# Other spare matmuls and another place for one group of products at the head of a fused mLSTM and two-layer MoE kernel

## The chip, the cores and the metric

The kernel runs on one core of a Trainium2 chip. The metric is the device time of one execution in microseconds. A run of the kernel before gives one time; the three that are known are 431.34, 433.4 and 435.36 us, the median is 433.4. One further execution was taken by the profiler; its span, from the first to the last instruction, is 429.5 us.

## The reference

An mLSTM runs over 768 steps for 2 batches of 8 heads with head size 40; its output, as 1536 tokens of 320 features, goes through two pairs of dense layers, 320 by 2048 and 2048 by 320, the first with a squared hinge, the second with a softplus.

```python
m_new = np.maximum(f_gate[:, :, t] + m, i_gate[:, :, t])
f_stab = np.exp(f_gate[:, :, t] + m - m_new)
i_stab = np.exp(i_gate[:, :, t] - m_new)
C = f_stab * C + i_stab * np.einsum('bhd,bhe->bhde', vt, kt)
n = f_stab * n + i_stab * kt
y[:, :, t] = sigmoid(o_gate) * einsum(C, qt) / maximum(abs(n . qt), 1)
...
g = np.where(h >= 1, h, np.where(h <= -1, 0.0, (h + 1) ** 2 / 4))     # h = x @ w_in
x = g @ w_out
...
g = np.maximum(h, 0.0) + np.log1p(np.exp(-np.abs(h)))                 # h = x @ w_in2
out = g @ w_out2
```

Inputs and outputs are float32. The weights arrive as 64-bit words and are turned into floats on the chip.

## The kernel before

The sequence is cut into 12 chunks of 64 steps; a chunk of both batches is 128 tokens. The maxima m come from two scans over the gates (L341): 256 steps (chunks 0 to 3, the early ones) and 512 steps (chunks 4 to 11, the late ones). For an early chunk the forget gates, a row for each head, are laid under a mask (`m`, L556), spread over 128 partitions by one product with `sel` (the spread, `bc`, L564) and turned into a triangular matrix of decays `f` by a scan on VectorE (L590). For a late chunk `f` comes by DMA from a scratch tensor (`scr_f`, L572) and is scanned at L598. `late` is the tile of the late chunks' gates; sixteen small products L422 (eight in the program, each in two passes), called the late maxima here, spread their maxima into bank D, three VectorE operations (L428) take them in, L432, L436 and L441 finish them, and two DMAs (L445) store them as `scr_d` and `scr_f`. The decay rows `dec` of the early chunks are stored from `gd` (L393) and read back on ScalarE's queue (L581).

A chunk's attention is, on TensorE, the scores (`qkp`, L518), the value product (`pv`, L505), the product with the state (`inner`, L511), the state's update (`stp`, L526) and three transposes of the result (L687); on VectorE the scores times the decays (L620), the query times the decay rows (L625), the denominator (L650, L653), the gated output (L657, L660), the state (L678) and the rest `xl` that the rounding to fp32r leaves (L698, L700); on GpSimd the scaled values `vi` and `ve` (L603, L613) and the state's decay (L669). `isp` (L399) are transposes that bring the input gates to the partitions.

The tokens form three blocks of 512 (chunks 0 to 3, 4 to 7, 8 to 11). A layer takes, for each of the 16 slices f of the hidden size, eight products up (L767), a few element operations, and eight products down (L836 to L842; in the second layer twelve, L897 to L899). Each weight slice comes as `raw` (L709), is turned into floats on ScalarE (L715, L719) and VectorE (L726) and split into two fp32r parts `w` (L738, L747); `raw` has two buffers, so a slice is fetched once VectorE is done with the one before the last. The first product needs chunks 0 to 3 and the first slice.

While TensorE has nothing to do in the head, it runs fills (L460): 128x512 bf16 products of a constant, whose result nobody reads.

The order on every engine is made by a planner, the class Plan, when the program is built: each piece of work is added with a cost, its reads and writes, a due time or a place `at`, and Plan.run goes through time by its own estimates and emits what is ready and most urgent. It keeps its own idea of TensorE's clock (fast or not, `self.fast`, with `self.edge` the next moment at which it may change). Fills are taken when no other TensorE work begins within 0.15 us by that clock; once the idea is fast, and fills and products of the last WINDOW sum to more than KEEP of it, a fill is left out and the engine left free for IDLE. After the first product no more are emitted. A task's `hold` is the planner's time before which it isn't chosen; on the chip nothing waits for it. What the chip does wait for are the data, and the order: each engine takes its instructions in the order in which they were emitted.

## Time and profile before

| | |
|---|---|
| median of three runs | 433.4 us (431.34 to 435.36) |
| span of the profiled execution | 429.5 us |
| TensorE (PE) busy | 409.7 us, 95% |
| VectorE (DVE) busy | 295.2 us, 69% |
| ScalarE (ACT) busy | 260.1 us, 61% |
| GpSimd (POOL) busy | 37.2 us, 9% |
| share of the chain that ended last | PE 77%, DMA 8%, DVE 6%, ACT 4% |

The time of the profiled execution itself, with what lies around its span, is not given; only the span is. PE is TensorE's products, PEld its weight loads, which overlap the products. Ends of products are modelled, so a row for several products is a little longer than the distance to the next one. "SPq" and "ACTq" are the queues of SyncE and ScalarE where DMAs are issued. A wait in brackets is the idle time of that engine in front of the row and what ended it.

### The profile page before, as it was taken

Reading aid. Unit: us, or ns where it says so; the run is one execution under the profiler, and the core shown is the slowest. Engines: PE = TensorE matmul, PEld = TensorE weight load, DVE = VectorE, ACT = ScalarE, POOL = GpSimd, SP = SyncE. Lnnn points to the kernel's source line nnn. Section 1 sums busy time; section 2 is a strip of 40 time slices with the busy share of each in tenths; the row PEclk is TensorE's granted clock in tenths of the full one; section 3 lists DMA queues with packets and bytes.
Section 4 is the critical chain, followed back from the end, with each engine's and each line's share of the span. In section 5 each row is a group of like instructions: output and inputs, shape, how many; then the busy total and the mean of one; then the engine's idle time right before and its main releaser. Section 6 shows DMA issues by size and latency. Waiting matters only on the chain.

```text
span 429.5 us, 8096 instructions
## 1 busy us (share of the span) xinstructions
PE 409.7 (95%) x3299; PEld 340.3 (79%) x3299; DVE 295.2 (69%) x479; ACT 260.1 (61%) x447; POOL 37.2 (9%) x46
## 2 busy tenths in 40 slices
PE   7988779999899999999999999999999999999994
PEld 5555558877788888887888888999989999899994
DVE  4687998999868556556878787655565555655552
ACT  3255867768666446889889755555555555555551
POOL 3333122213101000000000000000000000000001
PEclk9999969999999999999999999999999999999999
DMA  8979595797912001644344000000020000110002
GB/s 289 343 260 318 156 295 177 213 321 221 304 66 74 2 2 51 193 162 136 134 134 137 0 2 0 1 2 0 2 61 2 0 2 0 36 27 2 0 2 61
DMA packets 13685, 44.93 MB, mean 105 GB/s; under 512 B 2320, under 2 KB 3984, under 8 KB 13648
## 3 DMA queue, kind: packets, MB, share of 16 engines
q1 hardware_dynamic: 12832, 43.22, 31.2%
q10 hardware_dynamic: 752, 1.03, 0.9%
q8 instruction: 26, 0.43, 0.4%
q0 software_dynamic: 64, 0.16, 0.2%
q14 instruction: 11, 0.09, 0.1%
HBM read 42.36 MB, written 2.05 MB: 103 GB/s over the span
## 4 chain that ended last, share of the span: by engine, by line
PE 77%; DMA 8%; DVE 6%; ACT 4%; issue 1%; SPq 1%; POOL 0%; DVEq 0%; POOLq 0%
PE h L767 36%; DMA raw<-in_w_dram 5%; PE D L841 4%; PE D L840 4%; PE D L842 4%; PE D L897 3%; PE D L899 3%; PE D L898 3%; PE A L898 3%; PE A L899 3%; PE A L897 3%; PE D L836 2%; PE D L837 2%; DMA f<-scr_f 2%; ACT v L715 1%
## 5 line engine op out<-in xcount | busy, mean ns | idle before, releaser
L767 PE MATMUL h<-xh,w 128*128 128x512 f32 x576 | 182.6, 400 | 1.5 <-DVE w L747 1.1
L767 PEld LDWEIGHTS h<-xh,w 128*128 128x128 f32 x576 | 108.7, 189 | 26.8 <-DVE w L747 3.0
L820 DVE TENSOR_TENSOR gl<-u,gh 128x512 fp32r<-128x512 f32 x96 | 67.5, 704 | 39.6 <-ACT gh L816 38.4
L816 ACT CAST gh<-u 128x512 fp32r<-128x512 f32 x96 | 59.4, 619 | 46.7 <-DVE u L807 34.0
L767 PE MATMUL h<-xl,w 128*128 128x512 f32 x192 | 76.3, 397 | 1.4 <-DVE xl L698 1.4
L807 DVE TENSOR_TENSOR u<-u,e 128x512 f32<-128x512 f32 x48 | 33.3, 693 | 29.2 <-ACT e L803 29.2
L803 ACT ACTIVATE e<-e 128x512 f32<-128x512 f32 x48 | 30.3, 632 | 37.6 <-DVE e L798 37.6
L775 ACT ACTIVATE u<-h 128x512 f32<-128x512 f32 x48 | 28.5, 595 | 25.9 <-PE h L767 25.6
L767 PEld LDWEIGHTS h<-xl,w 128*128 128x128 f32 x192 | 36.4, 190 | 8.0 <-DVE xl L698 1.8
L784 DVE SCALAR_TENSOR_TENSOR u<-u,h 128x512 f32<-128x512 f32 x48 | 32.7, 682 | 13.9 <-ACT u L780 13.7
L841 PE MATMUL D<-gh,w 128*128 128x512 f32 x96 | 37.9, 395 | 0.0
L840 PE MATMUL D<-gh,w 128*128 128x512 f32 x96 | 37.8, 394 | 0.0
L842 PE MATMUL D<-gl,w 128*128 128x512 f32 x96 | 37.5, 391 | 0.0
L798 DVE SCALAR_TENSOR_TENSOR e<-u,h 128x512 f32<-128x512 f32 x48 | 33.0, 687 | 6.0 <-ACT u L794 1.0
L726 DVE SCALAR_TENSOR_TENSOR v<-raw,v 128x704 int32<-128x704 int32 x32 | 28.6, 895 | 9.8 <-ACT v L719 8.8
L794 ACT ACTIVATE u<-h 128x512 f32<-128x512 f32 x48 | 28.7, 598 | 10.6 <-PE h L767 10.3
L747 DVE TENSOR_TENSOR w<-v,w 128x64 fp32r<-128x64 f32 (+2 forms) x45 | 30.2, 701 | 2.4 <-ACT w L738 2.4
L715 ACT ACTIVATE v<-raw 128x704 f32<-128x704 int8 x32 | 27.1, 849 | 7.3 <-DMA raw<-in_w_dram 5.4
L780 ACT ACTIVATE u<-u 128x512 f32<-128x512 f32 x48 | 30.2, 630 | 0.4
L897 PE MATMUL D<-w,gh 128*128 128x320 f32 x96 | 29.6, 309 | 0.1
L899 PE MATMUL D<-w,gl 128*128 128x320 f32 x96 | 29.7, 309 | 0.0
L898 PE MATMUL A<-w,gh 128*128 128x320 f32 x96 | 29.7, 309 | 0.0
(120 smaller groups left out, 611.5 us busy)
## 6 DMA issues: line engine op xcount, KB each, us to landing
raw<-in_w_dram SPq DMA_DIRECT2D x32, 704.0 KB, 4.8
qx<-in_qk_dram SPq DMA_DIRECT2D x12, 640.0 KB, 7.2
tok<-in_tok_dram SPq DMA_DIRECT2D x12, 496.0 KB, 6.0
dec<-scr_d SPq DMA_DIRECT2D x16, 128.0 KB, 6.7
f<-scr_f SPq DMA_DIRECT2D x16, 128.0 KB, 6.7
out_dram<-o SPq DMA_DIRECT2D x20, 80.0 KB, 2.1
dec<-scr_d ACTq DMA_DIRECT2D x6, 128.0 KB, 7.0
consts<-in_ident_dram SPq DMA_DIRECT2D x1, 164.0 KB, 4.0
```

The costliest lines, as they stand in the source:

```text
L767: nc.tensor.matmul(hp, a, x, start=(i == 0), stop=(i == len(ops) - 1))
L784: nc.vector.scalar_tensor_tensor(out=tiles[U], in0=tiles[U], scalar=1.0, in1=tiles[HP], op0=ALU.min, op1=ALU.max)
L798: nc.vector.scalar_tensor_tensor(out=new("e", E, [128, n]), in0=tiles[M], scalar=-2.0, in1=tiles[HP], op0=ALU.mult, op1=ALU.add)
L807: nc.vector.tensor_tensor(out=tiles[M], in0=tiles[M], in1=tiles[E], op=ALU.add)
L816: nc.scalar.copy(new("gh", GH, [128, n], F32R), tiles[G])
L820: nc.vector.tensor_tensor(out=new("gl", GL, [128, n], F32R), in0=tiles[G], in1=tiles[GH].bitcast(F32), op=ALU.subtract)
L840: nc.tensor.matmul(d[i], hi[:, k], gh, start=s, stop=False)
L841: nc.tensor.matmul(d[i], lo[:, k], gh, start=False, stop=False)
L842: nc.tensor.matmul(d[i], hi[:, k], gl, start=False, stop=e)
L897: nc.tensor.matmul(d, gh[:, k], hi, start=s, stop=False)
L898: nc.tensor.matmul(d, gh[:, k], lo, start=False, stop=False)
L899: nc.tensor.matmul(d, gl[:, k], hi, start=False, stop=e)
```

## The change

Six lines of the planner's numbers and of two tasks' descriptions change; what is computed, and by which instructions, doesn't, but for the number of fills.

```diff
-    KEEP, IDLE = 0.8, 0.1
+    KEEP, IDLE = 1.1, 0.1
+    WARMUP = 6.9
...
-        self.fast, self.busy, self.edge = False, 0.0, self.WINDOW
+        self.fast, self.busy, self.edge = False, -1.0, self.WARMUP - self.WINDOW
...
-        ready = [t["hold"] for t in ts]
+        ready = [max(t["hold"], 0.0 if t["fill"] or t["eng"] != "pe" else self.WARMUP) for t in ts]
...
-    add("pe", 0.9, t, duty=0.75, reads=[(gm, 1), (gm, 0), (gi, 1), (("bc", 1),)], writes=[(("D",), "s")], at=-50.5)
+    add("pe", 1.75, t, duty=0.75, reads=[(gm, 1), (gm, 0), (gi, 1), (("bc", 1),)], writes=[(("D",), "s")], at=-50.5, hold=8.3)
...
-        add("pe", 0.25, t, fill=True, reads=[(("warm",),)], writes=[(("fill",),)], new=[("hb", ("fill",))] if i == 0 else [])
+        add("pe", 0.22, t, fill=True, reads=[(("warm",),)], writes=[(("fill",),)], new=[("hb", ("fill",))] if i == 0 else [])
```

By the planner's time no TensorE work but fills begins before 6.9; its idea of the clock may turn fast at 3.49 and then at 6.9; with KEEP at 1.1 no fill is ever left out; the late maxima cost it 1.75 in place of 0.9 and aren't chosen before 8.3. From these numbers the planner makes a new order on all engines. The number of fills goes from 40 to 54. From the third slice of block 1 on TensorE's order is what it was. The line added moves all later lines by one: L422 before is L423 after.

At the head of TensorE's order, behind five fills, there stood before (`qx_151` and `qx_157` are chunks 0 and 1, `bc_224` and `bc_256` their spreads):

```order
L518 MATMUL A<-qx_151 64x64 x16
L399 MATMUL isp_200<-consts,gi 128x16 x2
L422 MATMUL D<-gm,gi 128x65 x8
L460 LDWEIGHTS warm
L460 MATMUL fill<-warm 128x512
L564 MATMUL bc_224<-m_216,sel 128x512
```

and there stand now, behind nine fills and with three fills ahead of the first row (`bc_234` is the spread of chunk 0):

```order
L423 MATMUL D<-gm,gi 128x65 x8
L565 MATMUL bc_234<-m_216,sel 128x512
L519 MATMUL D<-qx_157 64x64 x16
L461 LDWEIGHTS warm
L461 MATMUL fill<-warm 128x512
```

The transposes `isp` and the scores of chunk 0 changed places ahead of those three fills. The late maxima stand directly ahead of the first spread, as before with a fill between. Four fills follow the last product shown, then the second spread.

On VectorE, from the third scan of a spread on, there stood before (`f_366` and `f_381` are chunks 2 and 3, `dec_120` and `dec_121` the decay rows of chunks 1 and 2):

```order
L590 SCALAR_TENSOR_TENSOR f_366<-bc_337,id_h 128x512
L657 SCALAR_TENSOR_TENSOR sig_339<-den_345,sig_339 128x320
L660 TENSOR_TENSOR y_372<-A,sig_339 128x320
L590 SCALAR_TENSOR_TENSOR f_381<-bc_374,id_h 128x512
L625 TENSOR_TENSOR qx_157<-qx_157,dec_120 128x512
L620 TENSOR_TENSOR f_366<-A,f_366 128x512
L625 TENSOR_TENSOR qx_220<-qx_220,dec_121 128x512
```

and there stand now (`f_310` and `f_362` are chunks 2 and 3):

```order
L591 SCALAR_TENSOR_TENSOR f_362<-bc_354,id_h 128x512
L658 SCALAR_TENSOR_TENSOR sig_351<-den_348,sig_351 128x320
L661 TENSOR_TENSOR y_384<-A,sig_351 128x320
L626 TENSOR_TENSOR qx_157<-qx_157,dec_120 128x512
L437 SCALAR_TENSOR_TENSOR late<-late 128x64
L442 MEMSET late 128x1
L621 TENSOR_TENSOR f_310<-A,f_310 128x512
L626 TENSOR_TENSOR qx_214<-qx_214,dec_121 128x512
```

The same operations stand ahead of the first L626, but for two masks (L557), which now stand earlier; the scan and the memset of the late rows moved from behind the second one to between the two. In the same order the 512-step scan of the maxima now stands ahead of the last two subtractions of the early gates, and the masks of chunks 1 and 2 ahead of the first scan of a spread (that of chunk 3 is on GpSimd).

On TensorE, behind the up products of slices 0, 1 and 2 of block 0, there stood before the down products of slice 0 and then chunk 4's attention; now there is this, and the down products of slice 1 follow (`f_548` is chunk 4, `w_0_578` slice 0):

```order
L506 MATMUL A<-vi_705,f_548 64x41 x16
L512 MATMUL A<-state,qx_439 64x41 x16
L519 MATMUL A<-qx_580 64x64 x16
L527 MATMUL A<-ve_725,tok_491 40x41 x16
L837 MATMUL D<-gh_0_0_738,w_0_578 128x512
L838 MATMUL D<-gl_0_0_758,w_0_578 128x512
```

Chunk 4's attention moved ahead of the first down products, and sixteen down products stand between it and its transposes, where none stood. On VectorE the scan of chunk 4 moved ahead of the first hinge.

## Rows read from the trace of the kernel before

**Rows 1.** Busy time by stretch (instructions in brackets), granted clock, DMA share
```profile
core 0: us, PE busy (x) PEld busy (x) DVE busy (x) ACT busy (x) POOL busy (x), PEclk, DMA share, GB/s
17.06:39.35 22.29, 18.74 (x458) 12.51 (x458) 20.89 (x44) 11.85 (x25) 9.19 (x11) 1.00 0.91 300
39.35:58.10 18.75, 13.49 (x171) 9.96 (x172) 15.46 (x27) 13.42 (x22) 3.27 (x3) 0.95 0.66 213
58.10:118.00 59.90, 57.75 (x712) 46.17 (x712) 54.28 (x95) 44.02 (x77) 12.78 (x14) 0.96 0.81 250
56.20:56.40 0.20, 0.00 (x0) 0.00 (x0) 0.17 (x2) 0.00 (x0) 0.00 (x0) 0.63 1.28 377
63.00:63.10 0.10, 0.10 (x2) 0.09 (x1) 0.10 (x1) 0.10 (x2) 0.00 (x0) 0.60 1.36 394
```

**Rows 2.** Chain of work that ended last, in time: start us, us, what
```profile
6.73 3.49 PE D L422 x16
...
11.19 1.31 PE fill L460 x3
...
16.48 0.75 PE fill L460 x3
...
22.46 0.67 PE A L518 x32
```

**Rows 3.** Timeline, TensorE: start us, us, line, operation, [idle before, what ended it]
```profile
1.92 2.32 PE L460 MATMUL fill<-warm 128*128 128x512 bf16 x5 [1.92 <-POOL warm L454]
...
39.35 0.50 PE L767 MATMUL h<-xl,w 128*128 128x512 f32 x1 [1.36 <-DVE xl L698]
...
50.01 0.68 PE L505 MATMUL A<-vi,f 64*64 64x41 f32 x32 [1.96 <-DVE f L620]
...
57.19 0.90 PE L687 MATMUL A<-consts,y 128*128 128x128 f32 x3 [2.85 <-DVE state L678]
```

**Rows 4.** Timeline, VectorE and, in the first row, ScalarE
```profile
4.99 0.41 ACT L369 ACTIVATE gi<-gi 16x256 f32<-16x256 f32 x1 [2.49 <-DVE gi L365]
5.22 1.27 DVE L341 TENSOR_TENSOR_SCAN gm<-gf,gm,gi 16x512 f32<-16x512 f32 x1
...
11.22 1.22 DVE L590 TENSOR_TENSOR_SCAN f<-bc,id_h 128x512 f32<-128x512 f32 x1 [2.67 <-PE bc L564]
...
14.56 1.22 DVE L590 TENSOR_TENSOR_SCAN f<-bc,id_h 128x512 f32<-128x512 f32 x1 [2.12 <-PE bc L564]
...
17.06 0.69 DVE L620 TENSOR_TENSOR f<-A,f 128x512 f32<-128x512 f32 x1 [0.74 <-ACT state L676]
17.67 1.28 DVE L556 TENSOR_TENSOR m<-gr,consts 128x512 fp32r<-128x512 f32 x2
...
22.90 0.67 DVE L625 TENSOR_TENSOR qx<-qx,dec 128x512 f32<-128x512 f32 x1
...
24.37 0.68 DVE L625 TENSOR_TENSOR qx<-qx,dec 128x512 f32<-128x512 f32 x1
...
27.55 0.28 DVE L436 TENSOR_TENSOR_SCAN late<-late 128x64 f32<-128x64 f32 x1
...
27.95 0.89 DVE L726 SCALAR_TENSOR_TENSOR v<-raw,v 128x704 int32<-128x704 int32 x1
...
29.90 0.42 DVE L698 TENSOR_TENSOR xl<-D,xh 128x256 fp32r<-128x256 f32 x1 [0.60 <-ACT xh L693]
...
42.58 0.69 DVE L784 SCALAR_TENSOR_TENSOR u<-u,h 128x512 f32<-128x512 f32 x1 [2.04 <-ACT u L780]
```

**Rows 5.** Decay rows' DMAs (L581): first two, then all four; issue and landing
```profile
L581 ACTq DMA_DIRECT2D dec<-scr_d x2: 520/561/602, 12.7 to 13.2; - x2
...
DMA to landing us min/median/max: 6.1/7.0/8.0
L581 ACTq DMA_DIRECT2D dec<-scr_d x4: 520/604/662, 12.7 to 14.6; - x4
...
DMA to landing us min/median/max: 6.1/8.6/9.3
```

## What I predict

> **What bounds the kernel now.** I read the page first: TensorE (PE) is busy 95% of a span of 429.5 us and three quarters of the chain that ended last are PE's. That is an average. From the third weight of block 1 on, some 126 us into the span, the change leaves the order of PE's work as it was, so it can act only before that. I therefore cut the time up to 118 us, behind which PE has work without a break, in three [rows 1]. From 17.06 to 39.35 VectorE (DVE) works 20.89 of 22.29 us: it paces the rest of the head. From 39.35 (where the first product's wait ends) to 58.10, DVE works 15.46 of 18.75 and PE only 13.49: each waits for the other. From 58.10 to 118 PE is at 57.75 of 59.90, DVE at 54.28: PE is the fuller, by little. What is won early counts only if it moves DVE's work or PE's products; a PE that is merely faster in the head is worth nothing by itself.
>
> Next I read PE's clock. The granted column says 1.00 from 0 on, but the durations say otherwise: a fill of 512 columns takes 0.437 us at 11.19 (three in 1.31) and 0.25 at 16.48 (three in 0.75) [rows 2]. So PE was at its 1.2 GHz level until about 16.4 us, after five fills (2.32 us) had been followed by a pause and by small products [rows 2, 3], and at 2.4 GHz afterwards. Later the granted clock itself is seen to fall and to come back: 0.63 over 56.20 to 56.40 puts the fall at 56.25, 0.60 over 63.00 to 63.10 the return at 63.08 [rows 1], 6.8 us at half speed, 3.4 us of PE's work, after PE had stood 2.85 us before the transposes of chunk 4 [rows 3].
>
> Last I read DVE's waits in the head [rows 4]: 2.67 us before the first scan of a spread (L590 at 11.22) and 2.12 before the second (14.56), both for L564 on PE. PE came late since the sixteen products of the late maxima (L422) took 3.49 us ahead of the first spread [rows 2].
>
> **The change, step by step** (lines as in the kernel before).
>
> *Nine fills in place of five.* At 2.32/5 us with the first one's tail, or 0.437 by the chain, nine take 3.9 us: 1.92 to 5.85. No row shows what nine do: after five of them the clock had not risen [rows 2, 3], and its one rise that the granted column shows, at 63.08 [rows 1], came in a run of transposes and products without a break since 57.19 [rows 3]. I take it that the clock is up at about 7 us, because nine fills are such a run and what followed the five, with pauses and small products, was not; the other case is the first rival. The Trainium skill (TensorE: Matmul & The Clock Gate, section "What's actually happening") says that the slow clock is the default, that sustained activity releases it, and that the moment differs from run to run because the chip's watch runs free of the kernel; so by the page the same nine fills may do it in one run and not in the next. If the nine do it the sum is that below; in the page's bad case it is 0.6 us less, and with what else can go wrong then the first rival.
>
> *What PE reaches when.* The order puts the 512-step scan of gm (1.27 us) ahead of the two subtractions, so the input gate's exponential, at 4.99 before [rows 4], starts about 1.6 us later (1.27, and some 0.3 for the other subtraction, which now also goes first) and ends, 0.41 long, at 7.0. The transposes L399 wait for it, and the scores of chunk 0, which went ahead of them, now stand behind them: 7.0 + 0.2, scores 0.67 [rows 2], three fills 0.75, the late maxima at 0.25/0.437 of 3.49 = 2.0, first spread 0.25 (it has a fill's columns). That is 10.9: DVE's first scan starts at 10.95 instead of 11.22, 0.3 earlier. Scores of chunk 1 0.67, four fills 1.0, second spread 0.25: 12.8 instead of 14.56. DVE is free for it some 0.25 us before (10.95, the scan of 1.22 and two short late rows), so 1.87 of the wait of 2.12 goes. The masks of chunks 2 and 3 (1.28 at 17.67) move to the time before the first spread and to POOL, and the wait of 0.74 for ACT before L620 goes. Together 0.3 + 1.87 + 1.28 + 0.74 = 4.2 us: DVE would be at the first decayed query (L625 at 22.90) at 18.7.
>
> *What is late next.* L625 needs the decay rows. They leave on ACT's queue at 12.7 to 14.6, which nothing in the change brings forward (their store waits for a scan that moves 0.3 us later, if at all), and land up to 8.0 us after issue for the first pair and 9.3 for the last [rows 5]: 13.2 + 8.0 = 21.2 and 14.6 + 9.3 = 23.9. So in the new order DVE stands for about 2.6 us before chunk 1's query, and chunk 2's starts at 24.0 against 24.37. Of 4.2 us, 0.35 are left. This step decides most of the sum. Behind it two smaller things hold: the late rows' scan and memset (27.55 to 27.95) now lie in that wait, 0.40; and the wait of 0.60 at 29.90 is filled, since chunk 3's L620 now stands ahead of L698. The first product comes 0.35 + 0.40 + 0.60 = 1.35 us earlier, at 38.0.
>
> *More fills in the head.* There are 54 fills instead of 40. PE cannot pass them. Seventeen stand round chunk 3's transposes and ahead of the first product, where eleven stood: six more, 1.5 us. Before, PE stood 1.36 us in front of the first product for DVE's last xl, at 39.35 [rows 3]. That wait covers all but 0.1, so I cost them at nothing; the cover gone, each costs 0.25, at the slow clock 0.44.
>
> *The order behind the head.* DVE takes the scan of chunk 4 (1.2 us) before it needs the first product's hinge, in the wait of 2.04 at 42.58 [rows 4]: 1.2 us gained, if that row's f and decay rows have landed. PE takes chunk 4's attention before the first down products and then two of these (16 products) before the transposes of chunk 4, so that they lie in what were waits of 1.96 and 2.85 us [rows 3]. DVE's idle time between 39.35 and 58.10 is 18.75 - 15.46 = 3.29 us. Beyond the 1.2 I count a third of the other 2.1, 0.7, since ACT feeds DVE there too. Bounds: 0 if the new order makes as many waits as it fills, 3.3 if it fills all.
>
> *The clock at 56 us.* With the 2.85 us wait filled the clock should not fall there. It is worth 0 to 3.4 us: 0 if DVE (54.28 of 59.90) paces what follows, 3.4 if PE does. I take 0, because products can't run ahead of the weights that DVE prepares, and keep 3.4 as a rival.
>
> **Sum:** 1.35 + 1.2 + 0.7 = 3.25 us. The profiled execution's span becomes 426.3 us. What lies around the span is not shown; its 429.5 is 3.9 below the median of the runs, 433.4, and I move the median by the same 3.2: **430.2 us**, 0.7% faster. A measurement of this kernel can tell about 1% from no change.
>
> **Rivals.**
> *The head's gain is swallowed, and the clock stays slow at first.* Then the late maxima take 3.49 and the first scan starts at about 13.8, 2.5 us later than before. Speaks for it: the 1.15 us in which PE stands behind the fills. But the decay rows cover most: chunk 2's query starts near 24.6, the first product 0.7 earlier. If the new order then also gains nothing, the time is 432.7. For that: every stretch after 39 has two or three engines close to full. 22%.
>
> *The clock's 3.4 us come on top.* For it: PE is the fuller engine from 58.10 on, and 4.98 of the slow microseconds lie there (to 63.08). 433.4 - 3.2 - 3.4 = 426.8. 22%.
>
> *Slower: the clock falls in the new wait for the decay rows.* No fill stands between chunk 2's scores and chunk 1's product with the state, which waits for L625, so PE stands there some 2.2 us; it stood 1.96 and kept its clock, and 2.85 and lost it [rows 3]. If it falls, the seventeen fills cost 0.19 more each, 3.2 us, or half of that if they themselves bring it back, 2.4 in the middle, and the first eight products 8 x 0.19 = 1.5: 433.4 - 1.35 + 2.4 + 1.5 = 436.0. It decides if PE stands nearer to 2.85 than to 1.96. 13%.
>
> *It does not do what it says.* In part it doesn't: the late maxima are to go behind the first spread, and the order has them still ahead of it. Had they gone behind, the first scan would start up to 2.0 us earlier and wait for the same decay rows; so this part is worth nothing either way and moves no chance.
>
> **How the numbers follow.** My forecast (428.5 to 432.5 alone) has 43%, the rivals 22, 22 and 13. Faster by over 1% (below 429.1): most of the second rival and the lower edge of the forecast, 0.32. Slower by over 1% (above 437.7): the far end of the third, 0.07. Within 1%: 0.61. The range runs from the second rival with the whole 3.3 us of DVE's idle time, 426.8 - 1.4 = 425.4 (3.3 less the 1.9 already counted), to the third, 436.0.
>
> **What would show it.** Right: fills of 0.25 us from about 7 us on; the two waits on L564 gone or below 0.5; DVE standing 2 to 3 us before the first L625 on a DMA, and the second L625 at 24 us; the first up product at 38 us; no granted clock below 1 at 56 us; 118 us reached some 3 us earlier. Wrong: the decay rows landing early, at 20 us or before (then up to 3.9 us more would be won), a slow clock between 20 and 40 us, or DVE's idle time between the first product and 58 us as large as before.

## The result, and the profile after

The change makes the kernel slower by a little. After it the median of 20 runs is 434.35 us (432.23 to 438.89); the kernel before, run beside it, has 431.69 us over 20 runs (429.59 to 437.44). The ratio is 1.0058, with a 95% interval of 1.0032 to 1.0085, or 2.5 us lost where 3.2 us of gain were forecast. The profiled execution took 434.4 us with a span of 432.6, so 1.8 us lie around the span; the 431.69 of before fits its span of 429.5 with the same 1.8, and the 433.4 on which the forecast was put was a high draw of three.

The stretches of the changed kernel first (rows of [rows 1] answer to them; the columns are the same). All line numbers are one higher than before.

```profile
core 0: us, PE busy (x) PEld busy (x) DVE busy (x) ACT busy (x) POOL busy (x), PEclk, DMA share, GB/s
8.00:8.80 0.80, 0.80 (x9) 0.21 (x3) 0.77 (x2) 0.49 (x3) 0.38 (x1) 0.90 0.99 393
8.80:9.00 0.20, 0.20 (x2) 0.20 (x2) 0.20 (x1) 0.00 (x0) 0.20 (x1) 0.50 1.01 363
17.06:39.35 22.29, 19.15 (x482) 13.23 (x481) 16.22 (x36) 9.54 (x19) 7.13 (x8) 0.96 0.80 258
18.50:19.00 0.50, 0.50 (x18) 0.50 (x14) 0.00 (x0) 0.50 (x1) 0.16 (x1) 0.61 1.13 336
39.35:58.10 18.75, 17.30 (x192) 12.26 (x191) 16.92 (x29) 13.16 (x25) 7.93 (x8) 1.00 0.68 194
58.10:118.00 59.90, 53.80 (x698) 41.08 (x698) 54.50 (x96) 45.72 (x79) 12.18 (x12) 1.00 0.80 249
```

The granted clock falls inside 8.00 to 8.80 (0.90) and comes back inside 18.50 to 19.00 (0.61): it is low from 8.65 to 18.89. (Ahead of the first rise the granted column says 1.00 too; the profile's record of the clock begins with that rise, here at 5.23, before at 15.29, where the prediction read some 16.4 from the fills.) At 56 us it no longer falls: 1.00 in both later rows. DVE, which paced the head with 20.89 of 22.29 us, now works only 16.22 there, so it stands. And from 58.10 to 118 PE is busy for 53.80 us where it was for 57.75; some 2.5 us of that difference are the clock, since before the first 4.98 us of this stretch ran at half speed [rows 1].

TensorE's timeline, as in [rows 3]:

```profile
1.92 3.74 PE L461 MATMUL fill<-warm 128*128 128x512 bf16 x9 [1.92 <-POOL warm L455]
7.15 0.29 PE L400 MATMUL isp<-consts,gi 16*128 16x16 f32 x2 [1.50 <-ACT gi L370]
...
8.81 3.67 PE L423 MATMUL D<-gm,gi 16*128 16x65 f32 x16
...
17.75 1.65 PE L527 MATMUL A<-ve,tok 64*64 64x41 f32 x32
...
43.89 0.50 PE L768 MATMUL h<-xl,w 128*128 128x512 f32 x1 [0.57 <-DVE xl L699]
...
59.55 0.55 PE L688 MATMUL A<-consts,y 128*128 128x128 f32 x3 [0.52 <-DVE y L661]
```

Behind the nine fills PE stands 1.50 us for the input gate's exponential; the late maxima take 3.67 us, as long as before (3.65 in the same view, 3.49 by the chain [rows 2]); the first up product's wait ends at 43.89, where it ended at 39.35. VectorE's timeline (and ACT's queue) against [rows 4, 5]:

```profile
13.24 1.22 DVE L591 TENSOR_TENSOR_SCAN f<-bc,id_h 128x512 f32<-128x512 f32 x1 [2.41 <-PE bc L565]
...
16.55 1.22 DVE L591 TENSOR_TENSOR_SCAN f<-bc,id_h 128x512 f32<-128x512 f32 x1 [1.81 <-PE bc L565]
...
19.52 0.69 DVE L621 TENSOR_TENSOR f<-A,f 128x512 f32<-128x512 f32 x1 [1.62 <-PE A L527]
...
27.31 0.68 DVE L626 TENSOR_TENSOR qx<-qx,dec 128x512 f32<-128x512 f32 x1
...
35.84 0.69 DVE L626 TENSOR_TENSOR qx<-qx,dec 128x512 f32<-128x512 f32 x1 [1.51 <-DMA dec<-scr_d]
```

```profile
27.53 1.12 ACTq L582 DMA_DIRECT2D dec<-scr_d  x2
```

The 4.5 us by which the first product is late are read off these rows. The first two scans of a spread are 2.0 us late (13.24 against 11.22, 16.55 against 14.56). The first scores times decays (L621) wait 1.62 us for the state product L527, which PE runs at the slow clock behind three slow fills: 2.5 us late (19.52 against 17.06), and chunk 2's query 2.9 (27.31 against 24.37). Chunk 3's decay rows are asked for at 27.53 in place of 25.69, and its query stands 1.51 us for them: that makes 4.5.

The later issue is only a part of that wait. The rows also take longer from issue to landing; first before, then after:

```profile
DMA to landing us min/median/max: 4.5/4.5/4.5
DMA to landing us min/median/max: 7.4/7.6/7.8
```

What SyncE's queue does ahead of them, before and, in the second fence, after:

```profile
18.78 2.82 SPq L490 DMA_DIRECT2D qx<-in_qk_dram  x2
```

```profile
25.62 0.33 SPq L446 DMA_DIRECT2D scr_d<-late  x1
...
26.50 0.90 SPq L491 DMA_DIRECT2D qx<-in_qk_dram  x2
```

In the new order the stores of the late rows stand ahead of the loads of two later chunks (`qx`, 640 KB each), and the queue waits for these rows (6.4 us in front of L446): the loads leave 1.0 us ahead of chunk 3's decay rows, where they had left 6.9 us ahead. So it is in every run below that has the changed head (they begin at 23.9 to 26.5 us) and in none with the head of before (18.6 to 20.1). In e1 and h1 chunk 3's decay rows left a little ahead of the loads and landed in 2.8 to 6.7 us, and its query didn't stand for them. That the loads make the landing slow is read from these rows; no run changes SyncE's queue alone in the head, so its share isn't shown.

Behind the head, waits of PE from 64 to 118 (columns: us in total, times, longest), before and after:

```profile
PE h L767 <- DVE w L747: 1.1, 1, 1.1
PE A L687 <- DVE state L678: 1.0, 1, 1.0
```

```profile
PE D L838 <- DVE gl L821: 2.1, 3, 1.4
PE h L768 <- ACT w L739: 1.6, 1, 1.6
PE h L768 <- DVE w L748: 1.2, 2, 0.9
PE A L688 <- DVE f L621: 0.5, 1, 0.5
```

By the products done in the two traces (a rough measure, since the two orders mix short and long products) PE is 5.0 us behind at 50, 1.8 ahead at 64, 3.4 behind at 100, and 3.1 behind from 118 to the end: the new order makes the head's loss good and gives it back while PE waits for weights (L739, L748) and for the hinge's rest (L821).

### The profile page after: what moved, and what is told of

Read it like the earlier page. It is cut to its first block, busy times and chain, and to the rows that moved or that the text cites. A ratio compares the mean times of both kernels' runs of the same rounds, so it can differ in the third digit from the quotient of the medians.

```text
span 432.6 us, 8116 instructions
## 1 busy us (share of the span) xinstructions
PE 412.6 (95%) x3313; PEld 339.8 (79%) x3313; DVE 295.6 (68%) x479; ACT 260.7 (60%) x447; POOL 39.5 (9%) x46
## 4 chain that ended last, share of the span: by engine, by line
PE 78%; DVE 8%; DMA 8%; ACT 4%; issue 1%; ACTq 0%; DVEq 0%
PE h L768 35%; DMA raw<-in_w_dram 5%; PE D L842 4%; PE D L841 4%; PE D L843 4%; PE D L898 3%; PE D L899 3%; PE D L900 3%; PE A L899 3%; PE A L900 3%; PE A L898 3%; PE D L838 2%; PE D L837 2%; DMA dec<-scr_d 2%; PE fill L461 2%; DVE v L727 2%
## 5 line engine op out<-in xcount | busy, mean ns | idle before, releaser
L768 PEld LDWEIGHTS h<-xh,w 128*128 128x128 f32 x576 | 107.7, 188 | 29.5 <-DVE w L748 3.5
L821 DVE TENSOR_TENSOR gl<-u,gh 128x512 fp32r<-128x512 f32 x96 | 68.3, 712 | 36.9 <-ACT gh L817 35.7
L808 DVE TENSOR_TENSOR u<-u,e 128x512 f32<-128x512 f32 x48 | 33.2, 692 | 29.3 <-ACT e L804 29.2
L785 DVE SCALAR_TENSOR_TENSOR u<-u,h 128x512 f32<-128x512 f32 x48 | 32.7, 681 | 12.8 <-ACT u L781 12.5
L727 DVE SCALAR_TENSOR_TENSOR v<-raw,v 128x704 int32<-128x704 int32 x32 | 30.8, 966 | 11.6 <-ACT v L720 10.5
L795 ACT ACTIVATE u<-h 128x512 f32<-128x512 f32 x48 | 28.7, 599 | 10.5 <-PE h L768 10.2
L748 DVE TENSOR_TENSOR w<-v,w 128x64 fp32r<-128x64 f32 (+2 forms) x45 | 29.4, 681 | 2.6 <-ACT w L739 2.5
```

The lines of the kernel that those rows point to most:

```text
L727: nc.vector.scalar_tensor_tensor(out=tiles[V], in0=mid, scalar=5, in1=tiles[V], op0=ALU.logical_shift_right, op1=ALU.bitwise_or)
L768: nc.tensor.matmul(hp, a, x, start=(i == 0), stop=(i == len(ops) - 1))
L808: nc.vector.tensor_tensor(out=tiles[M], in0=tiles[M], in1=tiles[E], op=ALU.add)
L821: nc.vector.tensor_tensor(out=new("gl", GL, [128, n], F32R), in0=tiles[G], in1=tiles[GH].bitcast(F32), op=ALU.subtract)
```

## The experiments

In all of them Plan.run is cut in two: `order` returns the list of tasks with their engines, by the old numbers (False) or the new ones (True), and `emit` emits it, so that a list can be cut, joined or changed. Line numbers are 11 to 14 higher than before. The table is the overview: where the first product with `xl` begins (39.35 before), where the granted clock is low between its first rise and 100 us, where the hinge of block 1's fourth slice begins (135.09 before; behind it all run alike), each in the profiled execution, and the ratio to the kernel before over all comparable runs.

| run | first xl product | clock up at; low | block 1's hinge | ratio (95%) |
|---|---|---|---|---|
| before | 39.35 | 15.3; 56.2-63.1 | 135.09 | 1 |
| after | 43.89 | 5.2; 8.6-18.9 | 138.19 | 1.0058 (1.0032-1.0085) |
| s1_head_before | 40.23 | 16.6; 47.3-50.7, 67.8-71.2 | 136.40 | 1.0023 (0.999-1.0056) |
| s2_head_after | 43.50 | 6.2; 9.6-16.4, 36.9-40.3, 60.8-64.2 | 137.84 | 1.0062 (1.0028-1.0097) |
| e1_no_break | 42.87 | 6.3; 26.8-33.6, 67.7-71.1 | 136.66 | 1.0035 (0.9999-1.007) |
| e2_gates_first | 40.91 | 4.8; 11.6-15.0, 28.7-32.1, 66.2-69.6 | 139.42 | 1.011 (1.0064-1.0157) |
| h3_gates_rest_before | 44.96 | 17.7; 38.1-41.5, 62.0-65.4 | 140.76 | 1.0039 (1.0-1.0077) |
| k3_five_fills | 44.08 | 17.6; 68.8-72.2 | 138.51 | 1.0104 (1.007-1.0139) |
| b1_nine_fills | 40.97 | 5.6; 9.0-12.4, 19.2-22.7, 29.5-32.9, 53.4-56.8 | 135.04 | 1.0018 (0.9988-1.0048) |
| l1_late_behind | 44.53 | 16.5; 23.3-26.8, 33.6-37.0 | 139.74 | 1.0081 (1.0047-1.0116) |
| r1_weights_early | 39.70 | 13.8; 58.2-61.6, 68.5-75.3, 99.2-106.0 | 149.40 | 1.037 (1.0316-1.0425) |
| c1_cut | 41.34 | 15.3; 28.9-32.3, 59.7-63.1, 66.5-73.3 | 141.78 | 1.0189 (1.0143-1.0235) |
| r2_loads_order | 39.52 | 15.3; 46.0-49.4 | 137.56 | 1.0065 (1.003-1.01) |
| h1_hold | 45.36 | 6.2; 57.4-60.8 | 139.25 | 1.0066 (1.003-1.0102) |
| h2_gates_hold | 44.94 | 7.3; 34.6-41.4, 61.9-68.7 | 141.19 | 1.0048 (1.0014-1.0082) |
| k1_split_fills | 43.89 | 16.5; 26.7-36.9, 60.8-67.7 | 142.01 | 1.0117 (1.0066-1.0167) |
| k2_few_fills | 42.66 | 6.5; 33.8-40.6, 54.2-57.7 | 136.21 | 1.0039 (1.0005-1.0072) |
| b2_hold | 40.72 | 6.9; 10.4-13.8, 58.1-61.6 | 135.41 | 1.0012 (0.9978-1.0046) |

The three columns in the middle are of one execution each, and single executions differ. Five of these traces have the head of before (before, s1, r1, c1, r2): in them the clock rises at 13.8 to 16.6 us and the first xl product begins at 39.35 to 41.34. The traced execution of h2, h3 and k1 is the slowest of its run, that of k2 is 1.5 us below the median of its run.

### Head or what lies behind it

The two orders are cut at the first up product and joined crosswise (s1 takes the head of before, s2 that of after):

```diff
-        plan.run(20.0)
+        first, second = plan.order(20.0, False), plan.order(20.0, True)
...
+        seq = first[:cut[0]]
+        done = {i for i, a in seq}
+        seq += [(i, a) for k, (i, a) in enumerate(second) if i not in done and not (i in fills and k < cut[1])]
+        plan.emit(seq)
```

> Order of the kernel before up to its first up product, order of the changed kernel behind it. Theory (the loss is made in the head): the first up product starts at 39.4 us as before, the order behind it then brings what the changed kernel showed between 39 and 64 us (from 4.5 us behind to 1.5 ahead), part of which is given back; 428.5 to 431.5 us beside 431.7 before, ratio 0.993 to 1.000. Rival (the order behind the head costs the time): ratio 1.006 or more.

> Order of the changed kernel up to its first up product, order of the kernel before behind it. Theory (loss in the head): the first up product at 43.5 to 44 us, 4.4 us late, and the order behind it makes good little of that; ratio 1.007 to 1.012, slower than the changed kernel. Rival (order behind the head costs the time): ratio 1.000 to 1.003.

The head of after with the rest of before gives 1.0062, as much as the whole change: the loss is made in the head. The rest of after behind the old head gives 1.0023, which can't be told from none and is not the gain of 1.9 us (0.9956) that the forecast had. Each of the two lies between what its theory and its rival gave, and their intervals overlap, so a small loss behind the head isn't ruled out. In s1's trace PE is 4.1 us ahead at 64 by its products, and 2.2 behind at 92; its waits between 64 and 118:

```profile
PE h L779 <- ACT w L750: 2.5, 1, 2.5
PE D L849 <- DVE gl L832: 1.7, 2, 1.4
PE A L699 <- DVE f L632: 0.6, 1, 0.6
PE h L779 <- DVE w L759: 0.3, 1, 0.3
```

These are 5.1 us where before had 2.1. The first of them takes most of the lead, and the clock goes with it:

```profile
66.66 0.50 PE L779 MATMUL h<-xh,w 128*128 128x512 f32 x1 [2.50 <-ACT w L750]
```

PE stands 2.50 us for a weight slice, the granted clock is low from 67.8 to 71.2, which at half speed is another 1.7 us of PE's work, and by the products PE is 0.8 behind at 72. e1 and e2 below lose a lead of about this size at the same product (stands of 2.0 and 3.4 us, clock low from 67.7 and 66.2).

### The clock in the head

e1 fills the stand behind the nine fills; e2 closes it by moving the 512-step scan back behind the two subtractions; h3 is e2's head with the rest of before; k3 leaves out four of the nine fills; b1 adds four fills to the kernel before.

```diff
 seq = plan.order(20.0, True)
+k = [i for i, a in seq].index(at["isp"])
+seq[k:k] = [(at["fill", i], []) for i in range(100, 107)]
```

```diff
 seq = plan.order(20.0, True)
+row = next(x for x in seq if x[0] == at["scan", 1])
+seq.remove(row)
+seq.insert([i for i, a in seq].index(at["gisub"]) + 1, row)
```

```diff
 seq = plan.order(20.0, True)
+drop = [at["fill", i] for i in range(5, 9)]
+seq = [(i, a) for i, a in seq if i not in drop]
```

```diff
 seq = plan.order(20.0, False)
+k = [i for i, a in seq].index(at["qkp", 0])
+seq[k:k] = [(at["fill", i], []) for i in range(100, 104)]
```

> The changed kernel with seven more fills behind its nine, so that PE does not stand the 1.50 us before the transposes of the input gate. Theory (that stand loses the clock): granted clock 1.00 from 5.2 us on through the late maxima, which then take 2.0 us instead of 3.7; the first spread starts at 10.5 to 11 instead of 12.4, the fills behind take 0.25 each; first up product at 39 to 40.5 us; ratio to before 0.994 to 1.000. Rival (the order itself costs, whatever the clock): clock held, but the first up product still at 42 us or later and the ratio 1.004 to 1.007. Third way: the clock falls at 8.65 all the same, since the small products let it fall; then all is as in the changed kernel.

> The changed kernel with the 512-step scan of gm moved back behind the two subtractions of the gates, as in the kernel before. Theory: the exponential of the input gate starts about 1.5 us earlier, PE goes from its nine fills into the transposes without standing, and the clock stays at 1.00 from 5.2 us; the first spread starts before 11.5 us, the first up product at 39.5 to 41, ratio 0.995 to 1.001. Rival (small products and the late maxima lose the clock, not the stand): the clock falls within 4 us of the rise, as at 8.65, and the ratio stays at 1.004 to 1.007.

> Head of the changed kernel with the 512-step scan moved back behind the two subtractions, the order of the kernel before from the first product on. With the changed order behind it this head was 4.1 us ahead at 64 and 4.3 behind at the end. Theory (the head costs what its first product is late, 0.7 to 1.5 us here, and the order of before hands it on): ratio 1.001 to 1.004. Rival (that head costs 4 us by itself): ratio 1.008 or more.

> The changed kernel with five fills ahead of the first real product, as before, in place of nine. Theory (the nine bring nothing here, since the clock falls before the late maxima): clock up at 15 to 20 us, first product within 1 us of 43, ratio 1.003 to 1.008. Rival (the early rise and fall itself makes the clock late): clock up by 16 us, first product at 41 or earlier, ratio 0.999 to 1.003.

> The kernel before with four more fills behind its first five, ahead of the scores of chunk 0: nothing else. Theory: clock up at 5.2 to 6.3 us and held through the late maxima (2.0 us in place of 3.5), first scan of a spread at 9.5 to 10.5 in place of 11.2, second at 12 to 13 in place of 14.6; the decay rows then hold the second decayed query at 24 us, and the first product comes 0 to 1 us earlier; ratio 0.996 to 1.001. Rival (the gain turns into PE standing for the decay rows, where the clock falls): granted clock 0.5 somewhere between 24 and 34 us, first product later than 39.4, ratio 1.002 to 1.006.

With the stand filled the clock holds, and the late maxima take the 2.0 us of the forecast. e1's rows on PE and, behind them, on DVE:

```profile
9.21 2.00 PE L434 MATMUL D<-gm,gi 16*128 16x65 f32 x16
...
25.82 0.39 PE L472 MATMUL fill<-warm 128*128 128x512 bf16 x1 [0.94 <-issue]
27.44 1.79 PE L538 MATMUL A<-ve,tok 64*64 64x41 f32 x29 [1.23 <-DVE xh L712]
...
31.72 2.60 PE L472 MATMUL fill<-warm 128*128 128x512 bf16 x7
```

```profile
21.88 0.69 DVE L637 TENSOR_TENSOR qx<-qx,dec 128x512 f32<-128x512 f32 x1 [1.29 <-DMA dec<-scr_d]
...
25.75 0.69 DVE L637 TENSOR_TENSOR qx<-qx,dec 128x512 f32<-128x512 f32 x1 [2.14 <-DMA dec<-scr_d]
```

DVE has y of chunk 0 at 20.1 in place of 21.4 and then stands 1.29 and 2.14 us for the decay rows; PE stands behind it (0.94 of that for nothing the profile names), the clock falls at 26.8 and seven fills take 2.60 us. So the first xl product is at 42.87, not at 39 to 40.5. The ratio, 1.0035, can't be told from the change's 1.0058. It is the rival that is nearly met (42 or later, 1.004 to 1.007): the clock was held where the loss was seen, and the loss moved on.

e2 and h3 run the same instructions up to the first product. The first rows are e2's, the second h3's:

```profile
6.41 0.29 PE L411 MATMUL isp<-consts,gi 16*128 16x16 f32 x2 [0.98 <-ACT gi L381]
...
8.02 1.99 PE L434 MATMUL D<-gm,gi 16*128 16x65 f32 x16
```

```profile
6.68 0.39 PE L412 MATMUL isp<-consts,gi 16*128 16x16 f32 x2 [0.74 <-ACT gi L382]
...
9.46 3.67 PE L435 MATMUL D<-gm,gi 16*128 16x65 f32 x16
```

In one execution the clock rose at 4.8, in the other, after the same nine fills, not before 17.7, and their first xl products lie 4.0 us apart. One trace of such a head is a draw. The ratios come from 6 and 12 runs: e2 is beyond what either theory gave; h3's ratio is in the range of its theory, though its first product is 5.6 us late and not 0.7 to 1.5. k3 shows that nine fills are not what hurts: with five the clock is up at 17.6 and the ratio is 1.0104, more than its theory gave (1.008 at most). In the order before nine fills (b1) bring a clock that rises at 5.6, falls three times in the head, and a ratio that can't be told from none; the fall between 24 and 34 us and the later first product are those of its rival.

### The late maxima behind the first spread

```diff
 seq = plan.order(20.0, False)
+row = next(x for x in seq if x[0] == at["late"])
+seq.remove(row)
+seq.insert([i for i, a in seq].index(at["bc", 0]) + 1, row)
```

> The kernel before with the sixteen products of the late maxima moved behind the first spread, the one thing that the change names and its order does not do. Theory (as forecast, worth nothing): first scan of a spread 1.3 to 2 us earlier (9.2 to 9.9), second unchanged at 14.5, first product within 0.3 us of 39.4, ratio 0.998 to 1.002. Rival (the first scan's lead carries through chunk 0's first state product): first product 1 us or more earlier, ratio 0.994 to 0.998.

Neither: it costs 0.8%. PE's first two rows, and DVE's second scan of a spread:

```profile
8.64 0.76 PE L577 MATMUL bc<-m,sel 128*128 128x512 f32 x1 [1.34 <-DVE m L569]
9.33 3.67 PE L435 MATMUL D<-gm,gi 16*128 16x65 f32 x16
```

```profile
16.46 1.23 DVE L603 TENSOR_TENSOR_SCAN f<-bc,id_h 128x512 f32<-128x512 f32 x1 [5.80 <-PE bc L577]
```

The first scan begins at 9.44, 1.8 us earlier, but PE now stands 1.34 us for the mask instead of doing the maxima meanwhile, so the second scan is 1.9 late; PE stands another 1.16 us at 21.8 with no releaser (see PE's own program), the clock falls twice in the head, and the first xl product is at 44.53. So the move that the change names is by itself, in the order of before, a loss.

### The order behind the head

r1 is s1 with every step of block 0's weights drawn forward to its place in the order before; c1 is the order before, but for the piece between the first and the fourth up product, which is the changed one; r2 is s1 with SP's queue, the loads, in the order before.

```diff
+rank[i] = min(k, spot[0][i] - 0.5) if i in wts and k >= cut[0] else k
```

```diff
+k = next(k for k, (i, a) in enumerate(second) if i == at["up", 0, 0, 3])
+mid = [(i, a) for i, a in second[:k] if i not in done and i not in fills]
...
+seq += mid + [(i, a) for k, (i, a) in enumerate(first) if i not in done]
```

```diff
+line = [i for i, a in first if plan.tasks[i]["eng"] == "sp"]
+for p, i in zip(line, line[1:]):
+    need[i].add(p)
```

> The kernel with the head of before and the order of the changed kernel behind it, in which every step of the weights of block 0 (load, ACT's and DVE's work) is drawn forward to the place that it has in the order before; chunk work and PE keep the changed order. In the run without this, PE was 4.1 us ahead at 64 us and 2.3 behind at 92, and ACT waited 6.9 us in all for loaded weights. Theory (the changed order puts the preparation of the weights behind the chunks' work, so the lead is given back): the lead at 64 is smaller (1 to 3 us), it is not given back; third weight prepared on DVE by 46 us (before 45.1, without this 48.8); ratio 0.994 to 0.999. Rival (DVE and ACT are full between 58 and 118, so what goes first costs the other): the lead is gone at 64 and the ratio stays at 1.000 to 1.004.

> Head of before, the order of the changed kernel up to its fourth up product (chunk 4's attention ahead of the first down products, scan of chunk 4 ahead of the first hinge), the order of before behind that. Theory (the early part of the new order gains some 4 us by 60 us, the later part loses it): lead kept in part, ratio 0.993 to 0.999. Rival (the lead is borrowed from the weights, so it is paid back whatever order follows): lag of 0.5 to 2 us at 92 and after, ratio 1.001 to 1.005.

> Head of before and the order of the changed kernel behind it on PE, DVE, ACT and POOL; only SP's queue (the loads) stands as in the kernel before, so that the weights' loads go ahead of the loads of chunks 5 and on. Without this ACT waited 6.9 us in all for loaded weights, and the fourth and fifth weight were asked for at 53.9 and 57.5 us, 2.2 us after their buffers were free, behind a chunk's load that waited until 52.3. Theory (the new order of the loads makes the weights late): ACT's wait for loads under 4 us, PE's waits for weights between 64 and 110 shorter by 2 us or more, ratio 0.994 to 1.000. Rival (the loads are late since their buffers come free late; the queue only shows it): loads move by less than 1 us, ratio 1.001 to 1.005.

Joining the orders piecewise costs 3.7% and 1.9%: in r1 VectorE stands 10.1 us for ScalarE and ScalarE 10.0 for loaded weights between 39 and 118 us, in c1 PE stands 5.0 for the hinge. So these two say nothing of the lead of 4 us. r2 is the clean one, since only SP's queue differs from s1. ACT's waits for loaded weights between 39 and 118 us fall from 6.9 to 4.9 us (3.8 before), PE's stand of 2.50 us becomes 0.8, its clock doesn't fall there, and PE stays ahead until 80 us (1.2), so the loads' place did make weights late; but then DVE stands for the rows of f, whose loads went behind:

```profile
DVE f L611 <- DMA f<-scr_f: 3.1, 1, 3.1
```

and PE's waits for the hinge's rest (L833) grow from 1.7 to 5.0 us; by 96 PE is 1.4 behind. The ratio is 1.0065, beyond the rival's 1.005. DVE's work from 64 to 118 is much the same in before (48.4 of 54 us), after (48.7) and s1 (49.0). So much of s1's lead goes by the place of the loads, and with the loads put back other waits take it; why these grow stays open.

### PE's own program

In e1 PE stood 0.94 us and 0.89 us where no semaphore held it. h1 and h2 are to hold the clock through the head with 16 and 15 more fills in the places where PE stood (h2 with the 512-step scan moved back as in e2), and the rest of before.

```diff
+more("isp", 7, 100)
+more(("att", 1, "inner"), 2, 110)
+more(("att", 2, "stp"), 7, 120)
```

```diff
+more("isp", 5, 100)
+more("late", 2, 110)
+more(("bc", 0), 1, 112)
+more(("att", 2, "stp"), 5, 120)
+more(("att", 3, "inner"), 2, 130)
```

> Head of the changed kernel with 16 more fills: seven behind the first nine, two ahead of chunk 1's product with the state, seven ahead of the state product of chunk 2, where PE stood (0.8 and 1.2 us) in the run that had only the first seven; the order of before from the first product on. Theory (the clock alone makes the head late): granted clock 1.00 from about 6 us to the first product, which starts at 38 to 39.5 us; ratio 0.996 to 1.001. Rival (the head's order costs by itself: decay rows asked for later, state product ahead of the decay): clock held all the same, first product at 40.5 to 41.5, ratio 1.002 to 1.006.

> The same with the 512-step scan behind the two subtractions and 15 more fills (five ahead of the gate's transposes, two ahead of the late maxima, one behind them, five ahead of the state product of chunk 2, two ahead of chunk 3's product with the state); the order of before from the first product on. If both the clock and the scan's place matter: clock held from 5 us on, decay rows asked for by 12.7, first product at 38 to 39, ratio 0.994 to 0.999, faster than both kernels. If the clock falls in the head all the same: first product at 40 or later and ratio 1.002 or more.

In h1 the clock is at 1.00 from 6.2 us to 57, and the first xl product is the latest of all, 45.36, later than its theory and its rival gave; in h2 the clock falls at 34.6, and the second of its two cases holds (first product at 40 or later, ratio 1.002 or more). h1's rows:

```profile
25.78 2.33 PE L473 MATMUL fill<-warm 128*128 128x512 bf16 x10 [1.16 <-issue]
...
34.41 0.49 PE L518 MATMUL D<-vi,f 64*64 64x41 f32 x20 [1.29 <-issue]
...
42.21 1.02 PE L473 MATMUL fill<-warm 128*128 128x512 bf16 x4 [3.35 <-issue]
```

"issue" is time for which the profile shows no releaser. Counted in the trace's records (products, weight loads and the few waits for a semaphore), PE had run 705, 961 and 1217 instructions when it stood; in e1 705 and 1217, in h2 705 and 961, in s2 and h3 961, in e2 and k3 961 and 1473, in l1 449: 449 and a multiple of 256 each time. (A few later waits without a releaser, at 66 us in r1 and near 110 in others, don't lie at such counts and stay unexplained.) The page of h1 has the instructions of PE and a queue for instructions:

```profile
PE 411.6 (95%) x3329; PEld 339.8 (78%) x3329; DVE 296.0 (68%) x479; ACT 260.4 (60%) x447; POOL 37.8 (9%) x46
...
q8 instruction: 26, 0.43, 0.4%
```

PE has 6697 records in all; those behind the first 448 are 24.4 times 256, and the queue moved 26 packets, 16 KB each. The times of the packets settle what they are. In h1 the second, third and fourth end at 24.30, 33.03 and 40.50 us, and PE goes on at 25.77, 34.41 and 42.21. In all 17 stands at these counts, in eleven runs, PE goes on 1.25 to 1.71 us behind the end of the packet that is next in line; and at none of the counts from 449 to 1473, in none of the traces, does PE go past one sooner than 1.2 us behind the end of its packet. (The packet was not still under way in most of the stands, as k1's expectation below has it; it had just ended.) So PE waits for the next 256 instructions of its program. The packet starts only once PE has entered the block before, 0.8 to 9.1 us later: for the stand of 3.35 us 5.1 us later, at 39.48, when PE had stood since 38.86. The Trainium skill (Runtime: NRT & Kernel Launch, section "Instruction fetch mechanics") says that programs are fetched in blocks of 16 KiB, 256 instructions, and that a boundary's cost is mostly hidden. The size agrees with the trace; the cost is not hidden here, 0.3 to 3.4 us at each of these 17 boundaries.

k1 makes the suspected cost larger by itself (each fill as two halves, in the kernel before); k2 is h1 with only every third fill behind chunk 2's state product, and five there in place of seven; b2 is to hold the clock in the order before.

```diff
-            nc.tensor.matmul(
-                tiles["fill",].rearrange("p (k n) -> p k n", k=4), warm, warm[:, None, :].to_broadcast([128, 4, 128]),
+            for k in range(2):
+                nc.tensor.matmul(
+                    tiles["fill",].rearrange("p (k n) -> p k n", k=4)[:, 2 * k:2 * k + 2, :], warm,
```

```diff
+rest = [(i, a) for i, a in first[k:] if i in fills]
+first = [x for x in first if x not in rest or rest.index(x) % 3 == 0]
```

```diff
+more(("qkp", 0), 4, 100)
+more("late", 2, 104)
+more(("att", 0, "pv"), 3, 110)
+more(("att", 1, "pv"), 2, 114)
+more(("att", 2, "stp"), 3, 118)
+more(("qkp", 3), 2, 122)
```

> The kernel before with each of its 40 fills of 512 columns made as two of 256: the same columns, 80 instructions of PE more in the head (a load and a product each). In the runs with more fills PE stood 0.5 to 3.4 us where no semaphore held it, at its 449th, 705th, 961st, 1217th or 1473rd instruction, 256 apart, while a transfer of 16 KB of the instruction queue was under way. Theory (PE waits for its own program, and each instruction more brings it to the next block earlier): such waits appear, 0.5 us or more, at one or more of these counts, the first product is later than 39.4 us; ratio 1.001 to 1.006. Rival (the waits come from something else): no wait of this kind, ratio 0.998 to 1.001.

> The run with the clock held through the head, with only every third of the fills behind the state product of chunk 2 (38 instructions fewer ahead of the first product). There PE stood 1.2, 1.3 and 3.4 us for its program and its first product began at 44.9. Theory (the late head was those waits, not the order): the wait at the 1217th instruction is under 1 us or behind the first product, the first product starts at 39 to 41.5; ratio 1.000 to 1.004. Rival (the order of the head costs by itself): first product at 42 or later with the waits gone, ratio 1.004 to 1.008.

> The kernel before with four more fills ahead of its first real product and twelve in the places where PE stood in the run that had those four alone (two ahead of the late maxima, three and two ahead of the first two products with the decay, three ahead of the state product of chunk 2, two ahead of the scores of chunk 3). Theory: clock held from 5.6 us through the head, but PE reaches its program's blocks earlier and waits there; first product at 39 to 41, ratio 1.000 to 1.004. Rival (a held clock pays): first product at 38 to 39, ratio 0.995 to 0.999.

k1 is slower by 1.2% (0.7 to 1.7, from six runs), 5 us, for 80 instructions whose columns are the same. Its rows:

```profile
1.92 2.32 PE L474 MATMUL fill<-warm 128*128 128x256 bf16 x10 [1.92 <-POOL warm L467]
...
26.79 0.45 PE L519 MATMUL A<-vi,f 64*64 64x41 f32 x6 [1.07 <-issue]
27.16 1.46 PE L474 MATMUL fill<-warm 128*128 128x256 bf16 x6
```

Ten halves take the 2.32 us of five fills [rows 3]. At 25.7 PE stands 1.07 us at its 705th instruction, in the middle of a value product; the clock then falls from 26.7 to 36.9, and the first xl product is 4.5 late. Chunk 2's query, ahead of the wait, is 0.55 late (24.92 against 24.37), the wait is 1.07, and most of the remaining 2.9 lies in the slow stretch behind it. In k2 the wait at 1217 is gone, one of 0.69 us at 961 is left, and the first xl product comes at 42.66, 2.7 us earlier than h1's and still 3.3 late. (Its expectation counts from the first up product of any kind, 44.9 in h1. That is 41.23 in k2, in the range of the theory, and 37.41 before, so it is 3.8 late.) What it stands for then are the decay rows, on DVE:

```profile
23.43 0.69 DVE L638 TENSOR_TENSOR qx<-qx,dec 128x512 f32<-128x512 f32 x1 [2.63 <-DMA dec<-scr_d]
...
34.60 0.69 DVE L638 TENSOR_TENSOR qx<-qx,dec 128x512 f32<-128x512 f32 x1 [1.95 <-DMA dec<-scr_d]
```

In the second of these waits PE stands too (1.47 us up to 32.80, then the 0.69), and the clock falls again (33.8). The rows of that second wait were asked for as early as before (25.79, before 25.69) and took 6.2 to 8.3 us to land where they had taken 4.5, with the loads of SyncE's queue 0.6 us ahead of them (25.23). So, as far as k2 tells, the head is late by its order too: what a held clock wins ahead of the decay rows is lost at them. b2, the most that a held clock gives in the order before (low only from 10.4 to 13.8), stands 0.81 us at 705 and has the time of the kernel before. No run was faster than the kernel before.

## Why the prediction was wrong

Forecast were 430.2 us, a range of 425.4 to 436.0 and a chance of 0.07 for slower by over 1%; 434.35 lies in the range, within 1%, and on the other side of no change. That it lies in the range is luck: the upper end is that of a rival whose mechanism did not come, and the whole was put on 433.4, 1.7 us above the median of before. The prediction said that order and clock each bring a little; the runs show the head costing 2.7 us (s2: 0.62% of 432) and the rest bringing nothing (s1: 0.23%, -0.1 to 0.56).

The term that failed is the head's 1.35 us, with the first product at 38.0: it came at 43.89, 4.5 us late in place of 1.35 early. The clock, which the sum takes to be up through the head, is where the trace first leaves the forecast; but it isn't the whole of it, since with the clock held past the first decay rows the product is still 3.3 us (k2) and 3.5 us (e1) late. The second term, 1.9 us behind the head, can't be told from none (s1). Which part of the head's order costs most stays open: the waits that the runs show there are for decay rows, for PE's own program and for slow products, not the same ones in each run.

- **The clock is up at about 7 us and stays.** Half right, and the step that failed first. It rose at 5.23; the 3.4 us that followed held a stand of 1.50, the transposes, the scores and three fills, and at 8.65 it fell, back only at 18.89. The prediction saw the stand (1.15 us) and counted it only as what speaks for the first rival, at 22%. Where it was filled (e1, h1, k2) the late maxima took 2.0 us as the sum had it, and the first two scans came at 11.6 to 11.8 and 13.5 to 13.6, against 10.95 and 12.8 in the sum. The Trainium skill (TensorE: Matmul & The Clock Gate, section "What's actually happening"), cited there, says that the moment differs from run to run; e2 and h3 agree, with 4.8 and 17.7 us for the same head.
- **Rival 1, clock slow first.** Its mechanism came true (first scan 13.24, its figure 13.8); its price did not. It had the first product 0.7 us earlier and 432.7; the product was 4.5 late. The term mis-sized is "the decay rows cover most": chunk 2's query began at 27.31, with no wait for decay rows at all. The prediction moved DVE's rows by the spreads alone; it overlooked that L620 also stands behind the state product L526, which writes into the same chunk's bank and came late behind slow fills (1.62 us), and it has no term for chunk 3's decay rows, which left 1.84 us later on ACT's queue and took 7.4 to 7.8 us to land in place of 4.5 (a wait of 1.51 us).
- **The decay rows decide** (21.2 and 23.9). Right where the clock held, and mis-sized: e1's queries began at 21.88 and 25.75, k2's at 23.43 and 25.20. Their loads left 0.3 to 0.7 us later (12.93 in after, 13.3 in e1, 12.66 before), the scan ahead of them having moved back behind the 512-step scan, and the last took 10.4 us to land in e1 against 9.3 [rows 5].
- **More fills cost nothing.** True of the changed kernel, which has no wait for its program above 0.3 us; but the reason given, a cover of 1.36 us, was not the point. What a fill can cost are its two instructions: k1 shows 5 us for 80 of them, b2 nothing for 32.
- **The late maxima behind the spread are worth nothing.** Wrong: in the order of before l1 loses 0.8%.
- **The order behind the head, 1.9 us.** Wrong. The waits named went (2.04 before the first hinge became 1.45, the 1.96 went, the 2.85 became 0.52), and PE was 1.8 us ahead at 64. From there to 118 its waits for weights and hinges rose from 2.1 to 5.4 us and took it back. The idle time of DVE was counted as if a filled wait stayed filled.
- **The clock at 56 us should not fall.** Right: 1.00. Its worth was taken as 0, and rival 2's 3.4 us did not appear: the products then wait for weights.
- **Rival 3, clock falls at the decay rows.** It did not in after, whose DVE came too late for such a wait. It did in e1 (26.8 to 33.6) and in k2 (33.8 to 40.6), where PE also stood for its program.

## What to carry to other kernels

A stretch of spare products that ended in a stand of 1.5 us and small products was worth nothing here: the clock that rose in it fell 3.4 us later. Before more of them are put into a head of small products, count PE's instructions as well as its time: at 256 to a block, a boundary was a possible wait of 0.3 to 3.4 us, and in k1 the slow clock behind it cost more than the wait. Look at every queue that a new order moves, not only at the engines: here loads that came to stand behind a late store went out with the rows that the next step waited for. And a lead in the middle counts only where what feeds the next stage has room: a lead of four us was gone at 72 us in s1 and e2 and at 96 in r2.

## What had not been expected of the hardware

PE waits for its own program when small products run at the full clock: 0.3 to 3.4 us at counts 256 apart, with up to 5.8 us in one head (h1: 1.16, 1.29 and 3.35), until 1.25 to 1.71 us behind the end of a packet of 16 KB. More fills and a held clock bring PE to a boundary earlier, and the packet doesn't come earlier by as much: PE had the 705th instruction behind it at 24.4 us in h1 and at 29.2 in after, the packet ended at 24.30 and 26.00. So the two gains work against each other. And the same first instructions saw their clock rise at 4.8 us in one execution and at 17.7 in another, with the first product 4.0 us apart.
